# Retention attention and a mixture of experts on one core: expert 0's weight loads, the tile loads and the gating moved in the order of the attention loop

## The chip, the cores and the metric

The kernel runs on one core of a Trainium2 chip. The metric is the device time of one execution, in microseconds; the time before is the median of three runs, 705.89 us (702.37 to 708.29). The engines are TensorE (PE; its weight loads are shown apart, as PEld), VectorE (DVE), ScalarE (ACT), GpSimd (POOL) and SyncE (SP), which here only issues DMAs. Each engine works through its own list of instructions in order and waits on semaphores for the others; an instruction that waits holds up all that is behind it on its engine.

## The reference

Attention with decay, without a softmax, and then a mixture of experts in which each token goes to one expert of eight:

```python
def _attn_ref(q, k, v):                      # B, H, S, D = 8, 8, 576, 64
    scores = np.matmul(q, k.transpose(0, 1, 3, 2)) / np.sqrt(D)
    gamma = 1.0 - 2.0 ** (-5.0 - np.arange(H))
    rel = np.arange(S)[:, None] - np.arange(S)[None, :]
    Dmat = np.where(rel >= 0, gamma[:, None, None] ** rel, 0.0)
    return np.matmul(scores * Dmat, v)

def _moe_ref(x, w_gate, w_output_gate, w1, w2):   # x: 4608 x 512; E, F = 8, 1024
    logits = x @ w_gate
    e_idx = np.argmax(logits, axis=1)
    gate_w = softmax(logits)[np.arange(N), e_idx]
    eom = 1 / (1 + np.exp(-(x @ w_output_gate)))
    for e in range(E):
        mask = e_idx == e
        ye = np.maximum(x[mask] @ w1[e], 0.0) @ w2[e]
        out[mask] = gate_w[mask, None] * eom[mask, e, None] * ye
```

x is the attention's output, one row of 512 numbers per token.

## The kernel before

The 4608 tokens are 36 tiles of 128 (NTILE); nine tiles make two sequences of 576 (CPB = 9), and the attention is carried from tile to tile within a sequence by a state. The kernel has an attention loop over the 36 tiles and then a stage of experts. The order of all instructions is written out by hand: each engine executes its part in the order in which the program text issues it.

**A step of the attention loop** (lines 470 to 500), for tile g. load(g + 3) (L258) puts the load of a tile's q, k and v, "pk", on SP's queue; pk has four buffers. scores(g + 1) (L313) multiplies q by k on TensorE into two of three PSUM banks, and VectorE masks them into S_sb (L317). GpSimd scales q of tile g + 2 (prep_q, L279) and v of tile g + 1 (prep_v, L284). out_x(g) (L344, L347) multiplies by the state and by S_sb on TensorE, and ScalarE copies the result, xT, out of PSUM (L352). update(g) (L330, L332) brings the state forward, k_rows(g + 1) (L291, L298) transposes k on TensorE and copies it on ScalarE. x_rows(g) (L358, L361) transposes xT on VectorE into a buffer "xq", of which there are two, and puts four stores of 64 KB on SP's queue, which write the tile's rows to xs in DRAM.

**Gating** runs on groups of four tiles, GT = 4, from the step four tiles after the group's first. In its first step the logits are multiplied on TensorE (L368) and gate_a finds the largest (L371 to L390, VectorE, with an exponential on ScalarE). gate_b in the second step counts tokens per expert (L400 to L407); gate_c in the third lets TensorE add the ranks (L413, L414), works out each token's slot in its expert's list (L419 to L432) and queues four scatters (L442, GpSimd), of which `some` issues one or two per step. In the kernel before all this stands behind x_rows in its step, and VectorE waits in its place for logits and ranks issued in the same step.

**Expert 0's weights.** In every fourth step, g % 4 == 3, load_w (L127 to L140) puts the load of a weight tile of 512 KB, "st" (three buffers), on SP's queue and at once issues its split into a high and a low part: a cast on ScalarE (L134) and a subtraction in two halves on VectorE (L139). Eight such tiles hold expert 0's w1 and w2.

**Into the experts.** After group SNAP = 5 the list of expert 0 holds enough tokens for its first 360 slots (NS = (360, 256): an expert's slots are worked in two parts, of three and two tiles). load_idx (L227, L230) reads the list back from DRAM, make_idx (L240) orders it, and gather_rows (L149) fetches the rows of three tiles of x. When the loop has ended, transp_pe (L178 to L183) brings each of the three into order on ScalarE (L180), transposes it on TensorE (L182) and splits it into xh and xl (L175, L176). Then come the logits of the last group, and expert 0's first matmuls (mm1, L202) between the last gating steps. mm1 multiplies x by w1 in three products of high and low parts; ScalarE applies the ReLU (L204) and VectorE forms the low part (L205). mm2 (L215) multiplies by w2, ScalarE scales (L218) and GpSimd scatters the rows to the output (L219). The second part of expert 0 and all later experts get their rows by gathers on GpSimd (L157), by lists that are complete only after the last scatter.

**Memory.** Pools on the left side are laid out in the order in which they are opened (lines 67 to 79): const, wpool (split weights), sm, wst, xg, xta (xh and xl of the first part), hpa (hidden rows of the first part).

Of the kernel before, what the change touches and what calls it, by code (L numbers as in the profile page):

```python
# [24 lines left out]
E = 8  # L25
# [5 lines left out]
NS = (360, 256)  # L31
CAP = sum(NS)
# [14 lines left out]
def tile_retention_moe(  # L47
# [21 lines left out]
    wpool = ctx.enter_context(tc.tile_pool(name="wpool", bufs=1))  # L69
# [8 lines left out]
    xta = mctx.enter_context(tc.tile_pool(name="xta", bufs=1))  # L78
    hpa = mctx.enter_context(tc.tile_pool(name="hpa", bufs=1))
# [21 lines left out]
    zw = const.tile([P, 512], F32, name="zw")  # L101
    stT = [const.tile([P, NP, D], F32, name=f"stT{i}") for i in range(2)]

    def load_rest(step):
# [3 lines left out]
        if step == 2:  # L108
            SP.dma_start(out=cbf_sb, in_=cbf)
            SP.dma_start(out=csm_sb, in_=csm)  # L110
            SP.dma_start(out=tok_sb, in_=tokid)
            SP.dma_start(out=cov_sb, in_=cov)
            NZ = E * NT // P // 3
            zl = const.tile([P, NZ, 2], I32, name="zl")
            G.memset(zl[:, :, 0:1], NT)
            G.memset(zl[:, :, 1:2], 0)
            for i in range(3):
                SP.dma_start(out=lst.rearrange("(i p r) w -> i p r w", p=P, i=3)[i], in_=zl)
            zr = const.tile([P, 4], F32, name="zr")
            G.memset(zr, 0.0)  # L120
            SP.dma_start(out=xs[NT:NT + 1, :].rearrange("a (p r) -> (a p) r", p=P), in_=zr)

            G.memset(lists, NT)
# [3 lines left out]
    def load_w(which, e, fp):  # L127
        src, W, shape = (w1, W1, [P, KB, 256]) if which == 1 else (w2, W2, [P, 2, DM])
        st = wst.tile(shape, F32, name="st")
        SP.dma_start(out=st, in_=src[e, fp].rearrange("p (a b) -> p a b", a=shape[1]))  # L130
        hi = wpool.tile(shape, F32R, name=f"w{which}h{fp}")
# [33 lines left out]
    def xt_of(e, part):  # L165
        if (e, part) not in XT:
            pl = pools[f"xt{part}"]
            XT[e, part] = (pl.tile([P, KB, NS[part]], F32R, name=f"xh{part}"),
                           pl.tile([P, KB, NS[part]], F32R, name=f"xl{part}"))
# [8 lines left out]
    def transp_pe(e, t, src):  # L178
        x = wk.tile([P, KB, P], F32, name="xq")
        A.copy(out=x.rearrange("p k (a i) -> p k a i", a=4), in_=XG[e, t].rearrange("p (a k i) -> p k a i", a=4, k=KB))  # L180
# [10 lines left out]
    def mm1(e, part, fb):  # L191
# [3 lines left out]
        hh = pools[f"ht{part}"].tile([P, n], F32R, name=f"hh{part}{fb}")  # L195
# [518 lines left out]
```

## Time and profile before

| what | before |
|---|---|
| median of three runs | 705.89 us (702.37 to 708.29) |
| the profiled execution, its own time | 710.61 us |
| its span, first to last instruction | 708.6 us |
| TensorE busy | 614.4 us (87%) |
| VectorE busy | 343.6 us (48%) |
| GpSimd busy | 329.6 us (47%) |
| ScalarE busy | 168.9 us (24%) |
| mean granted TensorE clock | 0.931 |
| moved by DMA | 94.44 MB, 133 GB/s over the span |

All rows of the trace belong to the one profiled execution. A row of the timeline gives start and duration in us, the engine, the line, the operation, what it writes and reads, and in brackets how long the engine stood before it and for whom; "POOLq", "SPq" and "ACTq" are the queues' own instructions, such as the issue of a DMA. A group's row gives the number of instructions, their busy time and the mean of one in ns, and then the idle time before them with its releasers. Matmuls are pipelined, so that their durations overlap and a busy TensorE need not be at its peak. The DMA share is the mean busy share of the core's 16 DMA engines.

### The profile page before, as it was taken

To read this page: it belongs to the slowest core of one execution; us is meant where nothing else is said; L and a number is where in the kernel's file an instruction comes from. 1 tells how busy PE (TensorE), PEld (TensorE's weight loads), DVE (VectorE), ACT (ScalarE), POOL (GpSimd) and SP (SyncE) were. 2 spreads that over 40 slices of the span, in tenths; PEclk is the share of its full clock that TensorE was granted. 3 is DMA by queue.
4 is the path that set the end of the run, shared out by engine and by line. 5 is a ranking of instruction groups with operands and counts; after the bars stand their busy time and mean duration, and the time that the engine had idled before them with its cause. 6 is when DMAs were issued, how large, how long until landed. Compare 5 with 4: busy or idle time off the path is not lost. (4 is left out here: it accounts for less than half of the span.)

```text
span 708.6 us, 13974 instructions
## 1 busy us (share of the span) xinstructions
PE 614.4 (87%) x5718; PEld 539.6 (76%) x5718; DVE 343.6 (48%) x693; ACT 168.9 (24%) x346; POOL 329.6 (47%) x343
## 2 busy tenths in 40 slices
PE   6866757866666599889999999999999999999996
PEld 4755646755555497869879979979979979979974
DVE  2355355574465542648727616625725734733500
ACT  1232132232222320322122212222222222222211
POOL 4346527536636325767427616625715724721011
PEclk9989877888979789999999999999999999999999
DMA  7667666867847204345315414513513621611001
GB/s 262 189 204 196 183 162 190 201 170 180 242 125 200 57 2 130 108 147 198 119 57 174 165 46 142 183 43 126 186 64 107 196 79 65 221 71 68 5 30 38
DMA packets 51139, 94.44 MB, mean 133 GB/s; under 512 B 11774, under 2 KB 33023, under 8 KB 51074
## 3 DMA queue, kind: packets, MB, share of 16 engines
q1 hardware_dynamic: 40786, 72.30, 34.4%
q0 software_dynamic: 9328, 19.93, 8.5%
q10 hardware_dynamic: 960, 1.31, 0.6%
q8 instruction: 45, 0.74, 0.4%
q14 instruction: 20, 0.16, 0.1%
HBM read 74.34 MB, written 19.86 MB: 133 GB/s over the span
## 5 line engine op out<-in xcount | busy, mean ns | idle before, releaser
L157 POOL DMA_INDIRECT x_q<-xs,gidx x148 | 164.3, 1110 | 53.4 <-issue 39.3
L202 PE MATMUL h_ps<-xh,w1h 128*128 128x360 f32 (+1 forms) x512 | 157.4, 307 | 3.4 <-ACT xh L175 3.4
L202 PE MATMUL h_ps<-xl,w1h 128*128 128x360 f32 (+1 forms) x512 | 156.9, 306 | 0.7 <-DVE xl L176 0.7
L202 PE MATMUL h_ps<-xh,w1l 128*128 128x360 f32 (+1 forms) x512 | 157.3, 307 | 0.0
L215 PE MATMUL y_ps<-w2h,hh 128*128 128x512 f32 (+1 forms) x320 | 126.8, 396 | 1.8 <-ACT hh L204 1.8
L215 PE MATMUL y_ps<-w2h,hl 128*128 128x512 f32 (+1 forms) x320 | 126.0, 394 | 0.0
L215 PE MATMUL y_ps<-w2l,hh 128*128 128x512 f32 (+1 forms) x320 | 125.8, 393 | 0.0
L219 POOL DMA_INDIRECT out_dram<-y,idx x40 | 40.8, 1020 | 182.3 <-ACT y L218 164.8
L313 PE MATMUL sc<-qs,pk 64*64 64x64 f32 (+1 forms) x1152 | 42.1, 281 | 72.3 <-DVE S_sb L317 37.7
L205 DVE SCALAR_TENSOR_TENSOR hl<-h_ps,hh 128x360 fp32r<-128x360 f32 (+1 forms) x128 | 59.1, 475 | 90.0 <-ACT hh L204 89.8
L202 PEld LDWEIGHTS h_ps<-xh,w1h 128*128 128x128 f32 x512 | 97.8, 191 | 4.8 <-ACT xh L175 4.1
L202 PEld LDWEIGHTS h_ps<-xl,w1h 128*128 128x128 f32 x512 | 98.1, 192 | 1.4 <-DVE xl L176 1.1
L202 PEld LDWEIGHTS h_ps<-xh,w1l 128*128 128x128 f32 x512 | 97.9, 191 | 0.0
L313 PEld LDWEIGHTS sc<-qs,pk 64*64 64x64 f32 x1152 | 34.4, 157 | 82.3 <-DVE S_sb L317 39.9
L204 ACT ACTIVATE hh<-h_ps 128x360 fp32r<-128x360 f32 (+1 forms) x128 | 54.4, 427 | 151.5 <-PE h_ps L202 150.4
L279 POOL TENSOR_TENSOR qs<-pk,gq_sb 128x512 f32<-128x512 f32 x36 | 46.1, 1281 | 92.6 <-DMA pk<-in_pack_dram 80.8
L215 PEld LDWEIGHTS y_ps<-w2h,hh 128*128 128x128 f32 (+1 forms) x320 | 58.9, 184 | 16.9 <-ACT hh L204 2.2
L215 PEld LDWEIGHTS y_ps<-w2h,hl 128*128 128x128 f32 (+1 forms) x320 | 58.8, 184 | 16.4 <-DVE hl L205 0.4
L215 PEld LDWEIGHTS y_ps<-w2l,hh 128*128 128x128 f32 (+1 forms) x320 | 58.8, 184 | 14.9
L176 DVE TENSOR_TENSOR xl<-x_t,xh 128x512 fp32r<-128x512 f32 (+1 forms) x37 | 24.9, 673 | 89.4 <-ACT xh L175 89.4
L218 ACT ACTIVATE y<-y_ps,idx 128x512 f32<-128x512 f32 (+1 forms) x40 | 27.5, 687 | 137.5 <-issue 96.9
L139 DVE TENSOR_TENSOR w1l<-st,w1h 128x1024 fp32r<-128x1024 f32 (+1 forms) x36 | 39.5, 1106 | 39.6 <-ACT w1h L134 36.7
(102 smaller groups left out, 682.6 us busy)
## 6 DMA issues: line engine op xcount, KB each, us to landing
st<-in_w_dram SPq DMA_DIRECT2D x64, 512.0 KB
pk<-in_pack_dram SPq DMA_DIRECT2D x35, 768.0 KB
xs<-xq SPq DMA_DIRECT2D x144, 64.0 KB
x_q<-xs,gidx POOLq DMA_INDIRECT x148, 3.3
gq_sb<-in_gq_dram SPq DMA_DIRECT2D x3, 256.0 KB
out_dram<-y,idx POOLq DMA_INDIRECT x40, 2.7
lst<-meta,sli POOLq DMA_INDIRECT x36, 5.8
pk<-in_pack_dram ACTq DMA_DIRECT2D x2, 256.0 KB
```

The lines of the kernel that those rows point to most:

```text
L139: V.tensor_tensor(out=lo[:, k], in0=st[:, k], in1=hi[:, k].bitcast(F32), op=ALU.subtract)
L157: G.indirect_dma_start(out=XG[e, t][:, u, :], out_offset=None, in_=xs.rearrange("t (a c) -> (t a) c", a=4), in_offset=bass.IndirectOffsetO ...
L176: V.tensor_tensor(out=lo, in0=src[:, :, 0:n], in1=hi.bitcast(F32), op=ALU.subtract)
L202: T.matmul(ps, lhsT=a[:, k, :], rhs=b[:, k, :], start=(j == 0), stop=(j == 3 * KB - 1))
L204: A.activation(out=hh, in_=ps, func=AF.Relu)
L205: V.scalar_tensor_tensor(out=hl, in0=ps, scalar=0.0, in1=hh.bitcast(F32), op0=ALU.max, op1=ALU.subtract)
L215: T.matmul(ps, lhsT=a[:, c0:c0 + n], rhs=b, start=(j == 0), stop=(j == 3 * FB - 1))
L218: A.activation(out=y, in_=ps, func=AF.Copy, scale=idx.bitcast(F32)[0:n, e, t, 1:2])
L219: G.indirect_dma_start(out=out, out_offset=bass.IndirectOffsetOnAxis(ap=idx[0:n, e, t, 0:1], axis=0), in_=y, in_offset=None, bounds_check= ...
L279: G.tensor_tensor(out=qs[g], in0=pk[g][:, 0].rearrange("p (n i) -> p n i", n=NP), in1=gq_sb[:, :, c0:c0 + P], op=ALU.mult)
L313: T.matmul(sc[r][64 * h:64 * h + 64, p, i], lhsT=pk[g][s, 1, P * p + 64 * h:P * p + 64 * h + 64], rhs=qs[g][s, p, i], start=True, stop=Tru ...
```

## The change

Six things are done.

- load_w is cut in two: load_w only loads, split_w splits. A weight tile is loaded at g % 4 == 2 and split at g % 4 == 0, two steps later, after prep_v and ahead of out_x.
- load(g + 4) takes the place of load(g + 3) and stands first in its step on SP's queue; four tiles are loaded ahead of the loop instead of three. The stores of x are taken out of x_rows into store_x, which stands one step later, behind the load.
- The logits and the ranks stay at the end of their step, but gate_a, gate_b and gate_c come a step after what they read, behind prep_v and ahead of out_x, and so ahead of x's transposition.
- k_rows is left out for the tiles whose k rows no update reads (the last of each nine).
- load_idx stands at step 31, make_idx and the three gathers at step 32. transp_pe is cut in order_x (ScalarE), transp_pe (TensorE) and split_x; the three gathered tiles pass through them in steps 34 and 35 and, the last split, behind the logits after the loop. The PSUM used is "kt" and two of the scores' banks.
- The fills of the lists go to the start, in a function fill, on VectorE instead of GpSimd; zeros and fill values use buffers of xq instead of their own.
- The pools wpool, xta and hpa are opened first, and the tiles of xta and hpa are widened from 360 to 384 columns (NW), one tile of the second part by 48 more, with only the first columns used.

```diff
 NS = (360, 256)
+NW = (384, 256)
+    wpool = ctx.enter_context(tc.tile_pool(name="wpool", bufs=1))
+    xta = ctx.enter_context(tc.tile_pool(name="xta", bufs=1))
+    hpa = ctx.enter_context(tc.tile_pool(name="hpa", bufs=1))
     const = ctx.enter_context(tc.tile_pool(name="const", bufs=1))
...
+    def fill(zl):
+        NZ = E * NT // P // 3
+        zl = zl.rearrange("p a c -> p (a c)").bitcast(I32)[:, 0:2 * NZ].rearrange("p (r w) -> p r w", w=2)
+        V.memset(zl[:, :, 0:1], NT)
+        V.memset(zl[:, :, 1:2], 0)
+        for i in range(3):
+            SP.dma_start(out=lst.rearrange("(i p r) w -> i p r w", p=P, i=3)[i], in_=zl)
+        zr = const.tile([P, 4], F32, name="zr")
+        V.memset(zr, 0.0)
+        SP.dma_start(out=xs[NT:NT + 1, :].rearrange("a (p r) -> (a p) r", p=P), in_=zr)
+        V.memset(lists, NT)
...
         st = wst.tile(shape, F32, name="st")
         SP.dma_start(out=st, in_=src[e, fp].rearrange("p (a b) -> p a b", a=shape[1]))
+        return which, e, fp, st
+
+    def split_w(which, e, fp, st):
+        W, shape = (W1, [P, KB, 256]) if which == 1 else (W2, [P, 2, DM])
         hi = wpool.tile(shape, F32R, name=f"w{which}h{fp}")
...
-    def transp_pe(e, t, src):
-        x = wk.tile([P, KB, P], F32, name="xq")
-        A.copy(out=x.rearrange("p k (a i) -> p k a i", a=4), in_=XG[e, t].rearrange("p (a k i) -> p k a i", a=4, k=KB))
+    def order_x(t):
+        x = XG[0, t, 1] = wk.tile([P, KB, P], F32, name="xq")
+        A.copy(out=x.rearrange("p k (a i) -> p k a i", a=4), in_=XG[0, t].rearrange("p (a k i) -> p k a i", a=4, k=KB))
+
+    def transp_pe(t, src):
         for k in range(KB):
-            T.transpose(src[:, k, :], x[:, k, :], ident)
-        split_x(e, t, src)
+            T.transpose(src[:, k, :], XG[0, t, 1][:, k, :], ident)
+        XG[0, t, 2] = src
...
+        hh, hl = (pools[f"ht{part}"].tile([P, NW[part] + 48 * (name == "hl17")], F32R, name=name)[:, 0:n]
+                  for name in (f"hh{part}{fb}", f"hl{part}{fb}"))
...
     for g in range(NTILE):
         S_sb = S_next
         prev = stcur[0] if g % CPB != 0 else None
-        if g < NTILE - 3:
-            load(g + 3)
+        if g + 4 < NTILE:
+            load(g + 4)
+        if g > 0:
+            store_x(g - 1)
         if g < 4:
             load_rest(g)
         n, late = divmod(g - GT, GT)
+        if g % 4 == 2 and g // 4 < 8:
+            wl.append(load_w(1 + (g // 4) % 2, 0, g // 8))
+        if g == 31:
+            load_idx(0, 1, 0)
         if g + 1 < NTILE:
             S_next = scores(g + 1)
+        else:
+            transp_pe(1, banks[0])
         if g + 2 < NTILE:
             prep_q(g + 2)
         if g + 1 < NTILE:
             prep_v(g + 1)
+        if late == 0 and wl:
+            split_w(*wl.pop(0))
+        elif n >= 0 and late > 0:
+            (gate_a, gate_b, gate_c)[late - 1](n)
+        if g == 32:
+            make_idx(0, 1, 0)
+            for t in range(TA):
+                gather_rows(0, t, (SNAP + 1) * GT * P)
+        if g == NTILE - 1:
+            split_x(0, 0, XG[0, 0, 2])
+            split_x(0, 1, XG[0, 1, 2])
+            order_x(2)
         out_x(g, S_sb, prev)
         update(g)
-        if g + 1 < NTILE:
-            k_rows(g + 1)
+        if (g + 1) % CPB != CPB - 1:
+            if g + 1 < NTILE:
+                k_rows(g + 1)
+        elif g + 1 == NTILE - 1:
+            order_x(0)
+            order_x(1)
+            transp_pe(0, ps_1.tile([P, KB, P], F32, name="kt"))
+        if g == NTILE - 1:
+            transp_pe(2, banks[1])
         x_rows(g)
-        if n >= 0:
-            if late == 0:
-                gt["ps"] = ps_1.tile([P, 512], F32, name="lg_ps")
-                logits(n, gt["ps"])
-                gate_a(n)
-            elif late == 1:
-                gate_b(n)
-            elif late == 2:
-                gate_c(n, ps_1.tile([P, 512], F32, name="lg_ps"))
-        some(2 if n >= SNAP else 1)
-        if g % 4 == 3 and g // 4 < 8:
-            load_w(1 + (g // 4) % 2, 0, g // 8)
-    for t in range(TA):
-        transp_pe(0, t, banks[t])
+        if n >= 0 and late == 0:
+            gt["ps"] = ps_1.tile([P, 512], F32, name="lg_ps")
+            logits(n, gt["ps"])
+        elif n >= 0 and late == 2:
+            ranks(n)
+        some(1 if g < 28 or g == 32 else 2)
     gt["ps"] = ps_1.tile([P, 512], F32, name="lg_ps")
     logits(NG - 1, gt["ps"])
+    split_x(0, 2, XG[0, 2, 2])
...
+    store_x(NTILE - 1)
     gate_a(NG - 1)
```

More of the change, by code (lines that the diff above doesn't have):

```diff
@@ L408, in gate_b, with ranks @@
         gt["b"] = (c1, zs)
-    def gate_c(n, ps):
-        (oh, ex), (c1, zs) = gt["a"], gt["b"]
+    def ranks(n):
+        oh, c1 = gt["a"][0], gt["b"][0]
+        ps = gt["r"] = ps_1.tile([P, 512], F32, name="lg_ps")
         r_ps = ps[:, 0:GT * E].rearrange("p (t e) -> p t e", t=GT)
@@ L510, in tile_retention_moe @@
     mm1(0, 0, 1)
-    gate_c(NG - 1, ps_1.tile([P, 512], F32, name="lg_ps"))
+    ranks(NG - 1)
+    gate_c(NG - 1)
     some(len(todo))
```

51 lines of the change are left out of this document (18 added, 33 removed).

## The prediction

> **What bounds the kernel now.** I read the page's slices first, then busy time by stage, then the waits of the first 250 us, then single rows of the order in time.
>
> ```profile
> span 708.6 us, 13974 instructions
> PEclk9989877888979789999999999999999999999999
> DMA  7667666867847204345315414513513621611001
> ```
>
> The slices are 17.7 us each. In the first fourteen (attention and gating) no engine is full, DMA is at six to eight tenths and the granted clock is below full; from the fifteenth on TensorE is full. By stage (duration; busy us of PE, PEld, DVE, ACT, POOL; clock; DMA share; GB/s):
>
> ```profile
> 0.00:16.00 16.00, 9.89 (x94) 6.22 (x96) 3.06 (x5) 1.87 (x2) 6.03 (x9) 0.90 0.82 290
> 16.00:238.00 222.00, 153.92 (x3087) 133.08 (x3083) 118.41 (x314) 62.12 (x131) 110.02 (x131) 0.83 0.67 182
> 238.00:250.00 12.00, 4.63 (x44) 3.24 (x44) 2.69 (x4) 3.73 (x7) 4.33 (x8) 0.65 0.18 34
> 250.00:708.00 458.00, 445.95 (x2503) 397.08 (x2499) 219.46 (x370) 101.16 (x207) 209.23 (x195) 0.99 0.32 107
> ```
>
> The 458 us of experts are 97% TensorE at clock 0.99. What the change touches is the 250 us before: a start of 16 us, the loop of 36 tiles, and a tail of 12 us with TensorE 39% busy. The waits from 16 us to 250 us (total, times, longest):
>
> ```profile
> POOL qs L279 <- DMA pk<-in_pack_dram: 78.5, 21, 7.4
> DVE w1l L139 <- ACT w1h L134: 36.7, 4, 10.0
> DVE w2l L139 <- ACT w2h L134: 33.1, 4, 9.5
> ACT w1h L134 <- DMA st<-in_w_dram: 28.9, 4, 7.8
> ACT w2h L134 <- DMA st<-in_w_dram: 28.3, 4, 8.3
> ```
>
> Eight times ScalarE stands at the cast of a weight tile whose load has only just been issued: 57.2 us. The copies of xT (L352), one per tile, are the loop's pulse; SP's and ScalarE's rows show a step with such a cast and one without:
>
> ```profile
> 16.09 0.58 ACT L352 COPY xT<-o_ps 128x512 f32<-128x512 f32 x1 [6.10 <-PE o_ps L347]
> 30.33 0.58 ACT L352 COPY xT<-o_ps 128x512 f32<-128x512 f32 x1 [5.69 <-PE o_ps L347]
> 34.79 0.47 SPq L130 DMA_DIRECT2D st<-in_w_dram  x1
> 39.67 1.04 ACT L134 CAST w1h<-st 128x1024 fp32r<-128x1024 f32 x1 [7.42 <-DMA st<-in_w_dram]
> 40.63 0.58 ACT L352 COPY xT<-o_ps 128x512 f32<-128x512 f32 x1
> 50.47 0.59 ACT L352 COPY xT<-o_ps 128x512 f32<-128x512 f32 x1 [0.71 <-PE o_ps L347]
> 54.00 0.59 ACT L352 COPY xT<-o_ps 128x512 f32<-128x512 f32 x1 [1.84 <-PE o_ps L347]
> 237.71 0.58 ACT L352 COPY xT<-o_ps 128x512 f32<-128x512 f32 x1 [1.03 <-PE o_ps L347]
> ```
>
> From the first copy to the last are 35 steps in 237.71 - 16.09 = 221.6 us, 6.33 us each. The step with the cast took 10.30 us (30.33 to 40.63), the undisturbed one 3.53 us (50.47 to 54.00). 35 x 3.53 = 123.6 us, so 98.0 us of the loop are waits: 57.2 us on weights and 78.5 us on pk, which partly lie over each other.
>
> **The change part by part.**
>
> *Weights two tiles ahead.* Load and cast are now two steps apart, at least 2 x 3.53 = 7.1 us; the load shown landed 39.67 - 34.79 = 4.9 us after its issue. I take the 57.2 us as gone. Cast (1.04 us) and subtraction remain, now ahead of xT's copy; TensorE's scores of the next tile cover them.
>
> *Tile load first, one tile more ahead.* Today the load of tile g+3 waits on SP's queue behind the four stores of tile g-1, which wait for VectorE's transposition, itself behind gating and the weights' subtraction. SP and GpSimd around tile 9:
>
> ```profile
> 70.35 0.38 SPq L258 DMA_DIRECT2D pk<-in_pack_dram  x1
> 71.62 1.75 SPq L361 DMA_DIRECT2D xs<-xq  x4
> 73.48 0.44 SPq L258 DMA_DIRECT2D pk<-in_pack_dram  x1
> 77.42 1.25 POOL L279 TENSOR_TENSOR qs<-pk,gq_sb 128x512 f32<-128x512 f32 x1 [6.51 <-DMA pk<-in_pack_dram]
> ```
>
> The first load was used 7.1 us after its issue, GpSimd having stood 6.5 us. With the load a tile further ahead and ahead of the stores, this latency fits into two steps; what remains is whether the DMA engines carry the bytes. A step moves 768 KB of pk, four stores of 64 KB and a quarter of 512 KB: 1152 KB, 1.18 MB.
>
> ```profile
> st<-in_w_dram SPq DMA_DIRECT2D x64, 512.0 KB
> pk<-in_pack_dram SPq DMA_DIRECT2D x35, 768.0 KB
> xs<-xq SPq DMA_DIRECT2D x144, 64.0 KB
> 20.00:40.00 20.00, 13.32 (x292) 11.30 (x290) 4.71 (x7) 4.60 (x11) 6.75 (x6) 0.91 0.80 246
> 103.00:118.00 15.00, 12.10 (x251) 10.39 (x240) 6.85 (x15) 3.10 (x8) 9.92 (x12) 0.89 0.84 273
> 54.00:58.00 4.00, 1.40 (x27) 1.10 (x26) 1.61 (x3) 1.47 (x3) 2.86 (x3) 0.91 1.01 323
> ```
>
> No stretch shows a queue that is never empty for long, so I bound the rate: 246 GB/s over 20 us gives 4.80 us a step, 273 over 15 us gives 4.32, 323 over 4 us with the engines full gives 3.65. I take the mean of the two long stretches, 4.56, as 4.6 us; the short one is one favourable mixture of loads and stores. The engines' own floors are below that:
>
> ```profile
> L279 POOL TENSOR_TENSOR qs<-pk,gq_sb 128x512 f32<-128x512 f32 x36 | 46.1, 1281 | 92.6 <-DMA pk<-in_pack_dram 80.8 <-DMA gq_sb<-in_gq_dram 11.0 <-PE o_ps L347 0.5
> L284 POOL TENSOR_TENSOR vs<-pk,gk_sb 128x512 f32<-128x512 f32 x36 | 37.4, 1039 | 2.7 <-DMA gk_sb<-in_gk_dram 2.3 <-PE st_ps L330 0.4
> L442 POOL DMA_INDIRECT lst<-meta,sli x36 | 36.2, 1006 | 30.1 <-DVE sli L432 24.9 <-issue 4.1 <-DVE bump L434 0.3
> ```
>
> GpSimd: 1.28 + 1.04 + 1.01 = 3.33 us, 0.11 us of gaps at the scatter (issue 4.1 / 36) and the small tick ahead of it: some 3.6. VectorE: 118.4 us over 35 steps, 3.4. TensorE: the 3.53 of the undisturbed step. ScalarE: 62.1 / 35 = 1.8. So the loop becomes 35 x 4.6 = 161.0 us, 60.6 less.
>
> *Gating ahead of x's transposition, logits and ranks a step earlier.* The same instructions; VectorE no longer stands for logits or ranks just issued. Queued behind them now is x_rows, and behind it the store on SP, no longer a load. It lies under the DMA's 4.6 us: nothing; uncovered, the 3.4 us of VectorE's work stand against 3.53, still nothing.
>
> *Start.* The fill's memsets move from GpSimd to VectorE before its first mask, and its 3 x 96 KB go out behind four tiles instead of three: 0.29 MB at the 290 GB/s of the start is 1.0 us, which I charge in full. Four k_rows whose result nobody uses go; they lie under DMA: nothing (uncovered, a small gain).
>
> *Tail.* Now:
>
> ```profile
> 246.47 0.62 ACT L180 COPY xq<-x_g 128x512 f32<-128x512 f32 x1 [2.54 <-DMA lst<-meta,sli]
> 248.19 1.94 PE L368 MATMUL lg_ps<-xT,wg_sb 128*32 128x128 f32 x32
> 250.05 0.67 PE L202 MATMUL h_ps<-xh,w1h 128*128 128x360 f32 x1
> ```
>
> From the last xT copy to the first expert matmul are 250.05 - 237.71 = 12.3 us: three gathered tiles reordered, transposed and split in turn. After, that work lies in the last two steps; behind the last copy stay its 0.58 us, the logits (1.94 at most), and one split, about 3.0 us. The two last steps gain some 2.5 us, since the reordering takes buffers whose stores must have landed (the third reordering stood 2.5 us). 5.5 us in all, 6.8 less; between 3 and 10 us. The gathers, three of about 1 us on GpSimd, come in one step instead of two; queued behind them on GpSimd is the scaling for tiles 34 and 35, for which the scores wait, with no load left to wait for: nothing, or 3 us.
>
> *Padding and order of pools.* Rows of xh and xl now begin every 1440 bytes, so k = 0 to 3 lie at four places within 256 B:
>
> ```profile
> 252.94 0.33 PE L202 MATMUL h_ps<-xh,w1h 128*128 128x360 f32 x1
> 253.44 0.32 PE L202 MATMUL h_ps<-xh,w1h 128*128 128x360 f32 x1
> 253.93 0.33 PE L202 MATMUL h_ps<-xh,w1h 128*128 128x360 f32 x1
> 254.41 0.33 PE L202 MATMUL h_ps<-xh,w1h 128*128 128x360 f32 x1
> ```
>
> Three matmuls per k take 0.50, 0.49, 0.48 us: the place is not visible. I price it at nothing; the spread, about 1% of 446 us to either side, is 4.5 us.
>
> *Sum.* Span 708.6 + 1.0 - 60.6 - 6.8 = 642.2 us; the profiled execution took 710.6, 2.0 more than its span: 644.2. It lies 4.7 us above the median of 705.9, so 639.5, forecast 640 us. With 4.3 to 5.0 us a step it is 629 to 654.
>
> **The rivals.**
>
> *The engines' floor.* DMA keeps 323 GB/s and the step is GpSimd's 3.65 us: 640 - 35 x 0.95 = 607 us; 607 to 629 with values between. For it: a rate seen with full engines. Against: only over 4 us, and TensorE must hold its full clock, which stood at 0.83 (3.53 / 0.83 = 4.25 us a step, 628 us). [...]
>
> *The pk waits stay.* Only the weights' waits go, all 78.5 us of pk lie on the path: 123.6 + 78.5 = 202.1 us of loop, 5.77 a step, 640 + 41 = 681; between 654 and 681 where part of them stays. For it: these waits are the larger sum. Against: at least 37.7 us of them lay over weight stalls (57.2 + 78.5 - 98.0), and the load's place on the queue is what the change moves.
>
> *The wait only moves to DMA.* If the loop's mean of 182 GB/s were all that this mixture gets, a step is 1.18 / 0.182 = 6.5 us, no shorter than 6.33 now; only the tail's 6.8 us less the start's 1.0 remains: 700. Against: a share of 0.67. [...]
>
> *Slower: stores behind loads.* x's stores are now queued behind a load, and xq has two buffers: x_rows(g+1) waits for the store of g-1. If the load takes the 7.1 us shown and the stores 4 us after it, 11.1 us must fit in some 1.75 steps: 6.3 us a step; every fourth step a weight load of 4.9 us ahead of the next tile adds 1.2. 7.5 x 35 = 263 us, 102 over the forecast: 742. It decides from the point where a store lands later than those 1.75 steps after its place on the queue (8 us at 4.6 a step), and VectorE would stand before x_rows for it. Against: 7.1 us was a load with another close behind it.
>
> **How the numbers follow.** Forecast 0.50, floor 0.20, pk waits 0.22, moved to DMA 0.04, slower 0.04. Range 612 to 676: it leaves out the ends of the two neighbours and the last two, about 0.2. A measurement tells about 1% from no change: faster by over 1% 0.92, within 0.04, slower 0.04.
>
> **What would show it.** Right: no wait of w1h or w2h on st; GpSimd's waits on pk below 40 us; xT copies 4.3 to 5.0 us apart with DMA share above 0.85 in the loop; the first expert matmul near 183 us, at most 7 us behind the last copy; 458 us after it, within 5. Wrong: a DMA share still below 0.75 with steps above 5.3 us (the order was not what held the loads), waits on stores, a clock near 0.8 with steps above 4.6, or an expert stage longer than 463 us.

## The result, and the profile after

The changed kernel took 647.37 us (median of four runs, 644.6 to 657.51) against 707.09 us of the kernel before beside it (702.37 to 713.62). The ratio is 0.9163, with a 95% interval of 0.9089 to 0.9236: 8.4% less time. The forecast was 640 us with a range of 612 to 676. The profiled execution took 648.10 us, of which its span is 646.3. Executions in a slower state (657.51 us here, 823.6 us in one run below) are in the medians and left out of the ratios.

The head of the page and its slices, now of 16.2 us each:

```profile
span 646.3 us, 13933 instructions
...
PE   6986988777569987999999999999999999999995
...
PEclk8998989898989998999999999999999999999999
DMA  9799988898531435462173155136217315511001
```

DMA is at seven to nine tenths through the first ten slices instead of six to eight, and TensorE is at seven tenths or more, nearly always nine, from the thirteenth slice to the last but one; before it was from the fifteenth on. By stage (duration; busy us of PE, PEld, DVE, ACT, POOL; clock; DMA share; GB/s):

```profile
15.00:195.00 180.00, 138.93 (x3080) 118.82 (x3076) 134.10 (x315) 60.08 (x132) 110.31 (x129) 0.92 0.80 222
...
199.00:646.30 447.30, 434.30 (x2488) 389.02 (x2486) 216.48 (x363) 100.76 (x206) 215.11 (x197) 0.99 0.33 110
```

The loop has gone from 222 to 180 us; the stage between loop and experts, 12 us before, is hardly there any more, and the experts are shorter too. The waits from 15 to 200 us (total, times, longest):

```profile
ACT zs L417 <- DVE zs L416: 39.5, 8, 6.7
ACT ex L396 <- DVE lm L393: 36.2, 8, 8.7
...
PE lg_ps L425 <- DVE c L412: 13.8, 6, 3.9
...
POOL lst L457 <- DVE x_g L155: 11.1, 1, 11.1
...
POOL qs L289 <- DMA pk<-in_pack_dram: 4.6, 4, 1.8
...
ACT w1h L141 <- DMA st<-in_w_dram: 1.9, 1, 1.9
ACT w2h L141 <- DMA st<-in_w_dram: 1.6, 1, 1.6
```

The two waits that filled the list before are gone: 78.5 us on pk are 4.6, 57.2 us on the weights are 3.5. At the top stand ScalarE's two exponentials of gating (L396, L417), for which it waits with the copies of xT (L362) behind them. The pulse of the loop:

```profile
14.84 0.58 ACT L362 COPY xT<-o_ps 128x512 f32<-128x512 f32 x1 [6.03 <-PE o_ps L357]
...
166.80 0.59 ACT L362 COPY xT<-o_ps 128x512 f32<-128x512 f32 x1 [0.85 <-PE o_ps L357]
171.65 0.58 ACT L362 COPY xT<-o_ps 128x512 f32<-128x512 f32 x1 [2.22 <-PE o_ps L357]
182.63 0.58 ACT L362 COPY xT<-o_ps 128x512 f32<-128x512 f32 x1 [0.42 <-PE o_ps L357]
190.27 0.57 ACT L362 COPY xT<-o_ps 128x512 f32<-128x512 f32 x1
194.53 0.59 ACT L362 COPY xT<-o_ps 128x512 f32<-128x512 f32 x1 [0.53 <-PE o_ps L357]
```

35 steps take 194.53 - 14.84 = 179.7 us. The first 31 take 152.0 us, 4.90 each; the last four take 27.7 us, one of them 11.0. The first expert matmul starts at 196.16, and the experts take 646.3 - 196.16 = 450.1 us instead of 458.5.

One of the long steps, on ScalarE, VectorE, GpSimd and TensorE:

```profile
54.76 0.57 ACT L362 COPY xT<-o_ps 128x512 f32<-128x512 f32 x1
62.80 0.20 ACT L417 ACTIVATE zs<-zs 128x4 f32<-128x4 f32 x1 [6.71 <-DVE zs L416]
62.91 0.57 ACT L362 COPY xT<-o_ps 128x512 f32<-128x512 f32 x1
54.97 3.00 DVE L400 TENSOR_TENSOR oh<-fst,m 128x32 bf16<-128x32 f32 x1
59.70 1.16 DVE L410 COPY c<-cum 128x8 bf16<-128x8 bf16 x1
60.89 1.35 DVE L412 TENSOR_TENSOR c<-c,oh 128x8 bf16<-128x8 bf16 x3
55.64 1.28 POOL L289 TENSOR_TENSOR qs<-pk,gq_sb 128x512 f32<-128x512 f32 x1
56.87 1.05 POOL L294 TENSOR_TENSOR vs<-pk,gk_sb 128x512 f32<-128x512 f32 x1
59.58 1.26 POOL L289 TENSOR_TENSOR qs<-pk,gq_sb 128x512 f32<-128x512 f32 x1 [0.47 <-DMA pk<-in_pack_dram]
60.80 1.04 POOL L294 TENSOR_TENSOR vs<-pk,gk_sb 128x512 f32<-128x512 f32 x1
62.30 0.19 PE L425 MATMUL lg_ps<-c,cbf_sb 128*128 128x32 bf16 x1 [3.88 <-DVE c L412]
```

Between the two copies of xT lie 8.15 us. L400, an operation on 32 elements per partition, took 3.00 us, to 57.97, and GpSimd's two scalings lay at 55.64 to 57.92; L410 took 1.16, to 60.86, beside a scaling that ended at 60.84. At 182.33 us, beside no scaling, L400 took 0.19 us. So these two operations of VectorE lasted until GpSimd's were over (L400 began 0.67 us ahead of the first scaling and stood all the same; the rows do not show why), ScalarE's exponential waits for it, xT's copy waits behind the exponential, and TensorE waits 3.88 us for the ranks' input.

### The profile page after: what moved, and what is told of

Read it like the earlier page. It is cut to its first block, busy times and chain, and to the rows that moved or that the text cites. A ratio compares the mean times of both kernels' runs of the same rounds, so it can differ in the third digit from the quotient of the medians.

```text
span 646.3 us, 13933 instructions
## 1 busy us (share of the span) xinstructions
PE 586.4 (91%) x5702; PEld 517.0 (80%) x5702; DVE 357.3 (55%) x697; ACT 163.7 (25%) x342; POOL 334.9 (52%) x339
## 5 line engine op out<-in xcount | busy, mean ns | idle before, releaser
L164 POOL DMA_INDIRECT x_q<-xs,gidx x148 | 169.7, 1147 | 53.2 <-issue 37.2
L211 PE MATMUL h_ps<-xh,w1h 128*128 128x360 f32 (+1 forms) x512 | 154.9, 303 | 2.0 <-ACT xh L181 2.0
L211 PE MATMUL h_ps<-xl,w1h 128*128 128x360 f32 (+1 forms) x512 | 154.9, 302 | 1.1 <-DVE xl L182 1.1
L211 PE MATMUL h_ps<-xh,w1l 128*128 128x360 f32 (+1 forms) x512 | 154.7, 302 | 0.0
L211 PEld LDWEIGHTS h_ps<-xh,w1h 128*128 128x128 f32 x512 | 96.2, 188 | 3.2 <-ACT xh L181 2.7
L211 PEld LDWEIGHTS h_ps<-xl,w1h 128*128 128x128 f32 x512 | 96.2, 188 | 2.0 <-DVE xl L182 1.7
L457 POOL DMA_INDIRECT lst<-meta,sli x36 | 37.2, 1033 | 55.8 <-DVE sli L447 29.0
L327 DVE TENSOR_TENSOR S_sb<-sc,cmat_sb 128x512 f32<-128x512 f32 x72 | 45.6, 673 | 26.6 <-PE sc L323 20.3
L323 PEld LDWEIGHTS sc<-qs,pk 64*64 64x64 f32 x1152 | 29.4, 140 | 32.7 <-POOL qs L289 14.2
```

The source lines that it names most:

```text
L164: G.indirect_dma_start(out=XG[e, t][:, u, :], out_offset=None, in_=xs.rearrange("t (a c) -> (t a) c", a=4), in_offset=bass.IndirectOffsetO ...
L211: T.matmul(ps, lhsT=a[:, k, :], rhs=b[:, k, :], start=(j == 0), stop=(j == 3 * KB - 1))
L323: T.matmul(sc[r][64 * h:64 * h + 64, p, i], lhsT=pk[g][s, 1, P * p + 64 * h:P * p + 64 * h + 64], rhs=qs[g][s, p, i], start=True, stop=Tru ...
L327: V.tensor_tensor(out=S_sb[:, r].rearrange("p (a b) i -> p a b i", a=2), in0=sc[r].rearrange("p (a b) i -> p a b i", a=2), in1=m, op=ALU.mult)
L457: i = G.indirect_dma_start(out=lst, out_offset=bass.IndirectOffsetOnAxis(ap=sli[:, t, :], axis=0), in_=meta[:, t, :], in_offset=None)
```

## Experiments

Theories: D, that the loop is now bound by the bytes that DMA moves; G, that it is bound by gating's waits in the engines' orders, the step above; and one question per part of the change. The ratios are against runs of the kernel before on the same chip; the runs were on several chips, so loops and stages are compared between traces. The loop is counted from the first copy of xT to the last, 179.7 us in the changed kernel and 221.6 before. Each loop is that of one execution; kernels that differ from the changed one only in the places of tiles gave 182.8 and 180.3 us, so a difference of some 3 us shows nothing.

### The exponentials at the end of ScalarE's step

```diff
-        A.activation(out=ex, in_=lm, func=AF.Exp)
+        gt["exp"] = partial(A.activation, out=ex, in_=lm, func=AF.Exp)
...
-        A.activation(out=zs, in_=zs, func=AF.Exp, scale=-1.0)
+        gt["exp"] = partial(A.activation, out=zs, in_=zs, func=AF.Exp, scale=-1.0)
...
+        if "exp" in gt:
+            gt.pop("exp")()
```

The last two lines stand at the end of the step.

> The changed kernel, but the two exponentials of gating are put on ScalarE's list at the end of their step, behind the copies of xT, of the state and of k, instead of ahead of them; nothing is left out. Theory G (the loop's 5.1 us a step come from ScalarE, which stands at these exponentials for VectorE's gating, with xT's copy behind it): ScalarE's waits at the two exponentials (66 us in the loop) no longer hold xT's copy, the steps with gate_a and gate_b fall from about 6 us towards 4.4, the loop from 180 us to 145 to 160, the time to 617 to 630 us. Theory D (the loop is bound by the DMA engines): the time stays within 6 us of 647 and GpSimd's waits on pk come back, over 25 us.

648.32 us, ratio 0.9137 (0.9061 to 0.9213): as the changed kernel. The loop took 178.3 us. The steps in which ScalarE had stood fell to some 3.5 us, and the steps behind them rose to 7 to 9, because TensorE now stood in them before the ranks (23.8 us in all for L412, 13.8 in the changed kernel). The 75.7 us of waits at the top of the list were worth nothing by themselves, so G's 145 to 160 us did not come. The time is D's, but D's waits on pk, over 25 us, did not come either: they were 11.6 us.

### And the ranks a step later

```diff
-        elif n >= 0 and late == 2:
-            ranks(n)
...
+        if n >= 0 and late == 3:
+            ranks(n)
```

They now stand behind the scores of the next step instead of at the end of gate_b's.

> The changed kernel with the exponentials at the end of their step, and the ranks put on TensorE's list one step later, behind the scores, ahead of gate_c. Theory R (the loop is held by VectorE's gating through two in-order waits, ScalarE's at the exponentials and TensorE's at the ranks): with both gone no engine waits for gating, steps near 4.3 us, loop 145 to 162 us, time 614 to 632 us. Theory D (the DMA engines, at a share of 0.9 in the loop, give no more): 640 to 650 us, with the waits back on pk or on x's stores, over 40 us together.

649.5 us, ratio 0.9125 (0.9029 to 0.9221); the loop 178.2 us. From 15 to 155 us:

```profile
15.00:155.00 140.00, 117.44 (x2588) 99.34 (x2585) 103.30 (x243) 49.77 (x104) 90.06 (x104) 0.89 0.95 248
```

DMA's share is 0.95 and its rate 248 GB/s, the rate of the changed kernel (248 over the same window at 0.89). Waits on pk (15.5 us) and on landed stores (14.5 us) come back as some of those on gating go, 30.0 us together where D expected over 40. This looked like D.

### GpSimd's scalings in four pieces

```diff
-        G.tensor_tensor(out=qs[g], in0=pk[g][:, 0].rearrange("p (n i) -> p n i", n=NP),
-                        in1=gq_sb[:, :, c0:c0 + P], op=ALU.mult)
+        for p in range(NP):
+            G.tensor_tensor(out=qs[g][:, p], in0=pk[g][:, 0, P * p:P * p + P],
+                            in1=gq_sb[:, p, c0:c0 + P], op=ALU.mult)
...
```

v is scaled in pieces likewise.

> The changed kernel with GpSimd's two scalings of a tile each cut in four instructions of 128 columns; the same results. Theory V (VectorE's short gating instructions stand until a GpSimd instruction of 1.0 to 1.3 us ends, which makes the steps with gate_a and gate_b 6 us long): those instructions last at most 0.4 us more than alone instead of up to 2.7, the loop is 10 to 20 us shorter, the time 627 to 640 us, unless the more instructions cost GpSimd itself over 0.5 us a step. Rival (something else holds them): the same durations, and a time of 647 us or more.

651.3 us, ratio 0.9197 (0.9124 to 0.927); the loop 176.9 us, 4.78 a step in the first 31. VectorE's groups from 15 to 195 us (count, busy us, mean ns), first of the changed kernel:

```profile
L400 DVE TENSOR_TENSOR oh<-fst,m 128x32 bf16<-128x32 f32 x8 | 8.0, 998 | 0.3
L410 DVE COPY c<-cum 128x8 bf16<-128x8 bf16 x7 | 7.5, 1073 | 0.0
```

then of this one:

```profile
L401 DVE TENSOR_TENSOR oh<-fst,m 128x32 bf16<-128x32 f32 x8 | 2.1, 266 | 0.3
L411 DVE COPY c<-cum 128x8 bf16<-128x8 bf16 x7 | 4.6, 660 | 0.0
```

With shorter GpSimd operations the same operation of VectorE takes 266 ns on average instead of 998 (the copy L410 660 instead of 1073). The longest shows the hold from its cause better than the mean: with whole scalings and late ranks the mean was 324 ns too, by where the scalings fell. It was 3.02 us in the changed kernel and is 0.8 us at most here, an estimate from the rows above: eight of 266 ns, less seven of the 0.19 us that it takes beside no scaling. Theory V expected a loop 10 to 20 us shorter and a time of 627 to 640 us, and neither came: the loop is 2.8 us shorter, no more than such loops differ by, and the time is that of the changed kernel. GpSimd was busy 121.98 us instead of 91.78 from 15 to 155 us, some 1.0 us more a step, over the 0.5 that the theory had named as its condition. So this run shows that the hold is there, but not what it costs.

### 256 KB more per step

```diff
+        dm = dram.tile([P, 512], F32, name=f"dm{g}")
+        SP.dma_start(out=dm, in_=pack[g, :, 0])
```

This copy from DRAM to DRAM is queued behind the stores; nothing reads it.

> The changed kernel with one more transfer of 256 KB per step, from DRAM to DRAM, behind x's stores on SP's queue; nothing reads it. Theory D (DMA bounds the loop): 0.26 MB at the loop's 222 to 260 GB/s are 1.0 to 1.2 us a step, the loop is 30 to 42 us longer, the time 677 to 690 us. Theory G (the exponentials' place): DMA has room, or can still hide most of it; under 12 us more, below 660 us.

671.45 us, ratio 0.946 (0.9375 to 0.9544), 24 us more; the loop 201.1 us. The window of the loop, and one wait of it:

```profile
15.00:165.00 150.00, 113.57 (x2441) 95.62 (x2439) 91.09 (x234) 44.27 (x99) 83.57 (x97) 0.89 0.96 265
```
```profile
DVE xq L368 <- DMA xs<-xq: 42.9, 20, 3.9
```

In the time, less than D expected (30 to 42 us) and more than G did (under 12). DMA can move more than 248 GB/s; VectorE waits for landed stores, as in the prediction's slower rival, with 42.9 us here against 5.4 in the changed kernel, and GpSimd waits 31.2 us for pk against 4.6.

### 256 KB less per step

Built on the kernel with late exponentials and late ranks, in which the waits on gating are smaller. The kernel leaves out v's loads, and GpSimd scales k's columns in v's place.

```diff
-        SP.dma_start(out=pk[g], in_=pack[g])
+        SP.dma_start(out=pk[g][:, 0:2], in_=pack[g, :, 0:2])
...
-        G.tensor_tensor(out=vs[g], in0=pk[g][:, 2].rearrange("p (h d) -> p h d", h=H),
+        G.tensor_tensor(out=vs[g], in0=pk[g][:, 1].rearrange("p (h d) -> p h d", h=H),
...
```

> The kernel with the late exponentials and late ranks, but v is not loaded: a tile's load is 512 KB (q and k) instead of 768 KB, and GpSimd scales k's columns in v's place, so all instructions of the engines stay. What is left out is v, so the gating routes other tokens; only the loop is to be read, not the experts' time. Bytes per step fall from 1.18 to 0.92 MB. Theory D (the loop is bound by what the 16 DMA engines move of this mixture, 242 to 248 GB/s): a step takes 0.92 / 0.245 = 3.75 us, 33 of them and the two long ones of 18.6 us make 142 us; loop 140 to 150 us, DMA share still above 0.85, rate near 245 GB/s. Theory I (the engines' orders of instructions bound it, DMA only fills along): loop 170 to 178 us, DMA share down to about 0.72, 190 GB/s.

The loop took 169.5 us, against 178.2 with v: the first 31 steps 4.55 us each instead of 4.88. (The whole time, 670.5 us, isn't comparable, since other tokens are routed.) From 15 to 155 us:

```profile
15.00:155.00 140.00, 119.58 (x2723) 100.81 (x2721) 122.35 (x260) 52.66 (x112) 97.39 (x111) 0.94 0.86 202
```

The loop is close to what theory I expected (170 to 178 us), though the share is not its 0.72, and D falls as a single bound: 0.26 MB less at 245 GB/s would be 1.07 us a step, and 0.33 came. The DMA share stayed at 0.86 although 19% fewer GB/s moved, so a share near 0.9 was no proof that the bytes bind. What rose most is VectorE, busy 122.35 of 140 us, 87%, against 103.30 (4.0 us a step against 3.6). Its one-hot operation again shows why:

```profile
L399 DVE TENSOR_TENSOR oh<-fst,m 128x32 bf16<-128x32 f32 x9 | 17.9, 1991 | 0.3
```

1991 ns for what takes 190 alone, since in this run both of GpSimd's scalings fall on it (one lasted from 52.17 to 55.05 us, the two scalings from 52.72 to 55.00); with v loaded it was 324 ns in the same order. So I read two limits close together: what DMA moves of this mixture, from 15 to 155 us 248 GB/s in the changed kernel and with late ranks and 254 with the scalings in pieces, and VectorE, held by GpSimd, at an estimated 4.5 us a step (4.55 in this run). Neither is shown alone. DMA moved 265 GB/s with the copy added, and in the row above TensorE is busy 119.58 us, 85%, beside VectorE's 87%, so which of them ends a step there stays open; a kernel with fewer bytes and a VectorE that is not held was not tried.

### No scatter behind the reading back of the list

The kernel with late exponentials and ranks, and no scatter issued in step 31:

```diff
-        some(1 if g < 28 or g == 32 else 2)
+        some(0 if g == 31 else 1 if g < 28 or g == 32 else 2 if g < 34 else 3)
```

> The changed kernel with both gating exponentials at the end of ScalarE's step, the ranks one step later, and no scatter issued in step 31, so that none stands on GpSimd's queue behind the reading back of the list (11.1 us in the changed kernel's trace, in its step 33 of 11.0 us). Theory D (bytes bound steps 1 to 31, the scatter's wait bounds 32 to 34): the loop before step 31 stays as with the late ranks (about 4.75 us a step, 245 GB/s); steps 32 to 34 come down from 18.6 us for the two long ones to about 10, so the loop becomes 169 to 172 us and the time 638 to 642 us, ratio 0.90. Theory G (the three gathers and their lists are what takes those steps, whoever waits): steps 32 to 34 keep their length, loop 178 us, 648 us.

643.91 us (641.01 to 650.54), ratio 0.9022 (0.8992 to 0.9052). The profiled execution is the slowest of the four (650.54), with a loop of 179.8 us whose last four steps took 27.9 us: the long step moved from 11.0 us before the third-last copy to 13.9 before the second-last. In the changed kernel these rows belong to it:

```profile
173.84 0.16 DVE L249 COPY idx<-lists 32x6 int32<-32x6 int32 x1 [1.97 <-DMA lists<-lst]
174.66 1.00 POOL L457 DMA_INDIRECT lst<-meta,sli  x1 [11.13 <-DVE x_g L155]
176.95 1.27 POOL L289 TENSOR_TENSOR qs<-pk,gq_sb 128x512 f32<-128x512 f32 x1
178.27 1.56 PE L323 MATMUL sc<-qs,pk 64*64 64x128 f32 x32 [4.61 <-POOL qs L289]
```

and in this one:

```profile
178.84 0.16 DVE L249 COPY idx<-lists 32x6 int32<-32x6 int32 x1 [2.24 <-DMA lists<-lst]
179.90 1.06 POOL L156 DMA_INDIRECT x_g<-xs,idx  x1 [9.28 <-DVE x_g L155]
184.95 1.26 POOL L289 TENSOR_TENSOR qs<-pk,gq_sb 128x512 f32<-128x512 f32 x1
186.26 1.56 PE L323 MATMUL sc<-qs,pk 64*64 64x128 f32 x32 [8.56 <-POOL qs L289]
```

In both, by the profile, GpSimd stands until the list is back, VectorE has ordered it (L249) and has cleared the first buffer for gathered rows (L155): 11.13 us before a scatter in the changed kernel, 9.28 us before a gather here. The scaling of the next q is queued behind, and TensorE stands 4.61 and 8.56 us before the next scores for that q. VectorE itself stands 2 us for the last piece of the list, with x's transposition behind it. This run's theory G holds for these steps: reading back and gathering take them, and GpSimd stands with or without a scatter there. The ratio's interval lies wholly below that of the changed kernel; but the two were not run on one chip, in microseconds they overlap (641.01 to 650.54 against 644.6 to 657.51), and the profiled execution doesn't show where a gain of some 3 us would lie. That stays open.

### Each part undone

The weights loaded and split at once, at g % 4 == 3:

```diff
-        if g % 4 == 2 and g // 4 < 8:
-            wl.append(load_w(1 + (g // 4) % 2, 0, g // 8))
...
+        if g % 4 == 3 and g // 4 < 8:
+            split_w(*load_w(1 + (g // 4) % 2, 0, g // 8))
```

> The changed kernel with expert 0's weights loaded and split at once at the end of every fourth step, as before the change; load first on the queue, gating and the rest stay. Theory W (weights were on the path with nearly all of their 57 us): ScalarE stands at the cast 40 to 57 us again, the time 680 to 700 us. Rival (the weights' waits lay over the pk waits, and with the loads a tile further ahead they cost less): 655 to 675 us.

672.5 us, ratio 0.9456 (0.9376 to 0.9535); the loop 203.5 us: the rival's time (655 to 675 us), not W's (680 to 700). ScalarE's casts wait 33.7 us, W having expected 40 to 57:

```profile
ACT w2h L141 <- DMA st<-in_w_dram: 18.6, 4, 6.3
ACT w1h L141 <- DMA st<-in_w_dram: 15.1, 4, 5.9
```

The load of tile g + 3 behind the stores, as before:

```diff
-        if g + 4 < NTILE:
-            load(g + 4)
         if g > 0:
             store_x(g - 1)
+        if g + 3 < NTILE and g > 0:
+            load(g + 3)
```

> The changed kernel with the load of tile g+3 behind the stores of tile g-1 on SP's queue, as before the change, instead of the load of tile g+4 ahead of them; weights, gating and the tail stay changed. Theory Q (the pk waits went because of the order on the queue): GpSimd stands for pk 40 to 80 us again and the time is 665 to 690 us. Rival (they went with the weight stalls and the gating, which had held the stores): waits on pk under 25 us and a time within 8 us of 647.

670.25 us, ratio 0.9427 (0.9347 to 0.9506); the loop 204.0 us, and the old wait is back, as theory Q expected, with a DMA share of 0.74 from 15 to 165 us:

```profile
POOL qs L289 <- DMA pk<-in_pack_dram: 62.7, 21, 8.1
```

Gating behind x's transposition, still a step after the logits, so that only its place in the step is undone:

```diff
-        elif n >= 0 and late > 0:
-            (gate_a, gate_b, gate_c)[late - 1](n)
...
         x_rows(g)
+        if n >= 0 and late > 0:
+            (gate_a, gate_b, gate_c)[late - 1](n)
```

> The changed kernel with gate_a, gate_b and gate_c behind x's transposition in their step (still a step after the logits; gate_c still behind ranks). In the run before with the exponentials moved, the loop stayed at 178 us because TensorE then stood at the ranks for VectorE's gate_b. Theory R (the count of gate_b, slowed by GpSimd, holds TensorE at the ranks of the same step wherever it stands): gating later on VectorE makes TensorE stand longer, 650 to 665 us. Rival (gating ahead of x's transposition is what costs): faster than 640 us.

673.51 us, ratio 0.951 (0.9444 to 0.9576); the loop 200.2 us: slower as theory R said, and by more (it had 650 to 665 us). TensorE, with the next scores behind, stands before the ranks for what VectorE does last in its step:

```profile
PE lg_ps L425 <- DVE c L412: 22.0, 8, 3.5
PE lg_ps L424 <- DVE oh L400: 16.3, 6, 4.8
```

Undone alone, each of the three parts costs 20 to 24 us of the loop, 68.6 us together (23.8, 24.3, 20.5), where all of them brought 41.9. They are not terms of a sum: each of the three, in its old state, holds a step at 5.5 to 5.6 us by itself (the mean of the first 31). Not undone alone were the k_rows left out, the place of the gathers, the fills, and the scatters of steps 24 to 27, now one a step instead of two.

### The weights alone, on the kernel before

```diff
-        if g % 4 == 3 and g // 4 < 8:
-            load_w(1 + (g // 4) % 2, 0, g // 8)
...
+        if g % 4 == 2 and g // 4 < 8:
+            wl.append(load_w(1 + (g // 4) % 2, 0, g // 8))
...
+        if late == 0 and wl:
+            split_w(*wl.pop(0))
```

> The kernel before with one change only: expert 0's weight tiles are loaded two tiles ahead of their cast. The profile of before has 98.0 us of waits in its loop, 57.2 us on the weights and 78.5 us on pk, partly over each other. Theory A (overlap, the waits on pk are what is left): the weights' waits go (under 5 us), those on pk stay near 78 us, and the loop shortens by 98.0 - 78.5 = 19.5 us: about 690 us, ratio 0.973. Theory B (the two add up, and each part of the change brings its own sum): 57 us come off, about 653 us, ratio 0.92. Theory C (a weight load's bytes only move to another place on the queue and hold pk's loads longer): pk's waits grow by as much, within 1% of before.

678.11 us, ratio 0.953 (0.9498 to 0.9562); the loop 187.1 us, 34.5 less than before.

```profile
POOL qs L283 <- DMA pk<-in_pack_dram: 37.9, 17, 8.1
ACT w1h L138 <- DMA st<-in_w_dram: 15.0, 4, 5.6
```

Between A (19.5 us off) and B (57), and for a reason that neither had: the waits on pk fell from 78.5 to 37.9 us without any change to pk's loads. The stall at the cast had held VectorE's subtraction, that the transposition, that the stores, and those the load of the next tile but two. SP shows it: it stood before the stores of x (L361) for VectorE for 123.9 us in the loop before, and for 72.6 (L365) here. Half of the pk waits were the weights' waits, one step later. And two steps of lead alone do not end the waits at the casts: 18.3 us stay (w1h 15.0, w2h 3.3), where A expected under 5.

### The old places

Pools in the old order, tiles 360 wide:

```diff
-NW = (384, 256)
+NW = NS
...
```

wpool, xta and hpa are opened where they were before, and no tile has 48 columns more.

> The changed kernel with the pools in the old order and the tiles of xta, hpa and the second part's hidden rows at their old widths (360 and 256 columns). Theory P (the places of the tiles within 256 B set TensorE's pace in the expert stage): matmuls of 512 columns follow each other every 0.232 us again instead of 0.228, those of 360 every 0.164 instead of 0.160, the expert stage is 6 to 8 us longer than 450, the time 653 to 656 us. Rival (the pace differs from execution to execution, or only the granted clock changed): the pace stays at 0.228 and 0.160, the time within 3 us of 647.

657.8 us, ratio 0.9255 (0.9179 to 0.933), 10 us more than the changed kernel; the experts take 456.9 us, 6.8 more, and the loop 182.8, 3.1 more. And only the widths (and the 48 columns), with the pools still first:

```diff
-NW = (384, 256)
+NW = NS
...
```

> The changed kernel with rows of xh, xl, hh and hl 360 elements wide again, without the 48 elements more in one of them; the pools of the weights and of part 0 stay first. Theory W (a matmul's pace goes by where its own streamed rows begin within 256 B): the matmuls with 360 columns, which stream xh and xl, go back from 0.160 to 0.164 us; those with 512 columns, which stream the weights W2, stay at 0.2276 us. Theory O (the order of the pools alone does it): all stay, 0.160 and 0.2276. Theory L (what counts is the place of the loaded weight against the streamed tile): those with 512 columns, which load hh and hl, go back to 0.232 us too.

652.06 us in one run; the experts 453.0 us. TensorE's matmuls of 512 columns (tile y_ps) from 260 to 600 us, with busy us and number: before,

```profile
260.00:600.00 340.00, 168.93 (x720) 131.71 (x720) 20.61 (x30) 0.99 0.37 120
```

after,

```profile
260.00:600.00 340.00, 164.92 (x720) 131.78 (x720) 21.32 (x31) 1.00 0.37 122
```

old places,

```profile
260.00:600.00 340.00, 172.32 (x738) 134.81 (x736) 22.03 (x32) 1.00 0.38 122
```

and old widths alone:

```profile
260.00:600.00 340.00, 169.16 (x725) 132.85 (x723) 21.32 (x31) 1.00 0.38 122
```

Per matmul that is 0.2346, 0.2291, 0.2335 and 0.2333 us. From start to start, worked out from the single rows, it is 0.2323 to 0.2328 us for all but the changed kernel, which has 0.2277. Those with 360 columns take 0.1607 in the changed kernel and 0.1641 with the old widths. With the old widths the ones with 512 columns go back too, although what they stream, w2, lies where it lay: what has moved is the loaded side, hh and hl. Theory L holds, with W for the 360 columns; the order of the pools alone does not do it for these two. That the place within 256 B is what counts, as the theories have it, was my assumption; the runs show only the widths and the order. The matmuls with 256 columns went the other way, from 0.117 to some 0.114 us with the old widths; why, and whether a layout has all three at their best, was not tried. For them the order counts: with the old places they take some 0.118 us, and 768 of them at 0.0048 us less are an estimated 3.7 us, nearly all of the 3.9 by which the experts of the two runs differ (456.9 and 453.0).

## Why the prediction was right, and where it was wrong

The range and the side were right, and the median lies 7.4 us above the forecast. Its terms against the trace:

| term | predicted | measured | difference |
|---|---|---|---|
| start, to the first copy of xT | 17.1 | 14.8 | -2.3 |
| 35 steps | 161.0 | 179.7 | +18.7 |
| last copy to first expert matmul | 5.5 | 1.6 | -3.9 |
| experts | 458.5 | 450.1 | -8.4 |
| span | 642.2 | 646.3 | +4.1 |

The sum is nearer than its terms: 18.7 us too little in the loop stand against 14.6 too much elsewhere, and that they nearly cancel is luck. Of the prediction's signs of being right two failed: the first expert matmul came at 196 us instead of 183, and the experts lie 8.4 us off instead of within 5.

**Weights two tiles ahead: right.** The waits went from 57.2 to 3.5 us, with the load first on the queue as well; without it 18.3 stayed. The weights alone brought 34.5 us of the loop. The rival "the pk waits stay" had all 78.5 us of pk left on the path, a loop of 202.1; the loop with the weights alone, 187.1, shows that half of them hung on the weights.

**The load first on the queue: right.** GpSimd's waits on pk are 4.6 us, and 62.7 with the old place.

**35 steps of 4.6 us: the mechanism half right, the size off.** In the first 31 steps it is 4.90, at 248 GB/s where I took the mean of 246 and 273. That is 9.4 us. A part is bytes: from the first copy to the 32nd DMA moved 250 GB/s, 1.23 MB a step, where I had counted 1.18. The lower rate that I averaged was met, but it isn't the DMA engines' limit: with 256 KB more a step DMA moved 265 GB/s, and with 256 KB less a step took 0.33 us less, not 1.07. Close below lies VectorE (TensorE, as said, is not ruled out), for which the prediction had 3.4 us a step. That figure came from a trace in which GpSimd stood 78.5 us for loads; with these gone more of VectorE's work falls beside GpSimd's scalings (the one-hot took 335 ns on average before, 998 now), and 109.02 us of VectorE from 15 to 155 us of the changed kernel are 3.8 a step, with the long ones in gating's steps. The row is this one:

```profile
15.00:155.00 140.00, 112.33 (x2519) 96.15 (x2519) 109.02 (x241) 47.17 (x103) 91.78 (x107) 0.92 0.89 248
```

The rival of the engines' floor, at 3.65 us a step, falls: the step took 4.90, and VectorE's part of it alone is 3.8, although the clock in the loop is 0.92 now instead of the 0.83 that spoke against it. That VectorE loses time to GpSimd's scalings the traces show: L400 ended at 57.97 us and the scaling at 57.92, and with the scalings in four pieces the longest L400 is an estimated 0.8 us at most instead of 3.02. By what mechanism was not shown.

**The gathers at step 32, "nothing, or 3 us": wrong.** The last four steps took 27.7 us instead of 18.4, the other 9.3 us of the loop's error. The mechanism was named rightly, the scaling queued on GpSimd and the scores waiting for it, but I had priced only the gathers' own time, not what GpSimd must stand for ahead of them: the list read back, put in order on VectorE and the buffers cleared. That was 11.13 us on GpSimd, of which 4.61 reached TensorE's scores in that wait alone; VectorE stood 2 us. With the weights alone, where this work still stood behind the loop, the last four steps took 20.4 us. So the tail's gain was partly paid for inside the loop: last four steps and tail together went from 22.7 + 12.3 = 35.0 us to 29.3.

**Gating ahead of x's transposition, "nothing": wrong.** Put back it costs 20.5 us of the loop and 3.0 of the tail. I had looked for its cost only on VectorE; the one who waits is TensorE, which has the ranks in front of the next scores.

**Start, 1.0 us more: not settled.** It was 1.3 us less in this execution, but in the other runs of the changed kernel with the same start the first copy of xT lies between 15.0 and 17.1 us, so neither my 1.0 us nor the 1.3 stands out.

**The tail, 5.5 us: shorter.** I had put 2.5 of it on the last two steps, which count in the loop above; against the other 3.0 stand 1.6, as the logits took 1.23 us instead of the 1.94 of before and the first expert matmul did not wait for the last split.

**Padding and order of pools, "nothing, within 4.5 us": wrong.** The experts became 8.4 us shorter and go back to 456.9 with the old places; the kernel before with only the weights moved has 456.7, so some 6.7 of the 8.4 are the places. I had compared matmuls at four places of k within one kernel, 0.48 to 0.50 us for three, and taken the place of the streamed row to be all that could matter; the gain with 512 columns (0.2277 us instead of 0.2323) came with the loaded tile.

**The slower rival** did not decide: VectorE waited 5.4 us for landed stores. Its mechanism is real, as 42.9 us with 256 KB more per step show.

## What to carry to other kernels

Undoing one part at a time and adding the losses counted 68.6 us where 41.9 were won: the engines work in order and hand their stalls on (with the weights alone moved, the waits on pk fell from 78.5 to 37.9 us), so a wait's total in the list is neither what its removal brings (75.7 us of ScalarE's waits were worth nothing, 28.3 + 28.9 us at the weights brought 34.5) nor independent of the others. A high DMA share and a steady rate do not show that bytes bind (0.95 and 248 GB/s with late ranks); taking bytes away tests it (0.33 us a step for 256 KB, not 1.07). An engine's floor read from a kernel full of waits is too low if its operations stretch beside another engine's (VectorE's 3.4 us a step before were 3.8 after), and work that is moved into a loop brings its waits with it, the reading back of a list included (11.13 us on GpSimd), for every engine that has something queued behind it.

## What the runs showed of the hardware

VectorE's one-hot operation (L400) took up to 3.02 us beside GpSimd's scalings in the changed kernel instead of 0.19; how much depends on where the scalings fall in the step (on average 335 ns before, 998 after, 324 with late ranks, 1991 with fewer bytes). Beside a gather that GpSimd was issuing (182.06 to 183.05 us) the one-hot took 0.19 us, and beside a scatter at 98.37 us too; it is the scalings that hold it. A matmul of 512 columns went at 0.2277 or 0.2323 us by where the tile that it loads lies (rows of 384 or 360 columns), 2%. Widths and order of pools together were worth 6.8 us of the experts, the widths alone 2.9 in one run.
